# Two FFN units taken in turns at the start of a fused attention and FFN kernel

## The chip, the cores and the metric

The kernel runs on one core of one Trainium2 chip, so its time is that core's device time in microseconds (us), and lower is better. The reported time is the median of unprofiled and profiled executions; the span in a profile is some 2 us shorter. Ratios are computed as the mean time of one kernel's fast runs over that of the other's of the same rounds, so they are not quite the ratios of the medians quoted.

## The reference, cut to what matters

Four batches of 12416 tokens of 128 channels. First an attention block with 32 inducing points, then a SwiGLU FFN with an RMS norm ahead of it:

```python
def mab(q, kv):
    s = scale * (q @ kv.transpose(0, 2, 1))
    s = s - s.max(-1, keepdims=True)
    a = np.exp(s)
    a /= a.sum(-1, keepdims=True) + 1e-09
    return a @ kv
h = mab(I, x)                      # I: the 32 inducing points
attn_out = mab(x, h)
...
rms = np.sqrt(np.mean(x * x, axis=-1, keepdims=True) + 1e-06)
xn = x / rms * rms_g
g = xn @ w_gate                    # 128 -> 1536
silu = g * (1.0 / (1.0 + np.exp(-g)))
return (silu * (xn @ w_val) @ w_out).astype(np.float32)
```

The FFN's weights arrive as 64-bit floats, and the kernel rounds them to 32 bits on the chip.

## The kernel before: the parts that matter here

The token stream is cut into 100 units of up to 512 tokens. A unit is twelve slots (j), one for each 128 of the 1536 FFN channels. In a slot, TensorE makes a gate product g and a value product v from the unit's tile a, ScalarE makes silu(g), VectorE makes u = silu * v, and TensorE adds u's product with w_out to acc a few slots later. Some slots split u in high and low parts instead (three cheaper products, on xn tiles). All attention work of the next batch is hung into these slots by slot number.

```python
for j in range(NJ):
    g = ps_gv.tile([P, 512], F32, name="gv", tag="gv")
    nc.tensor.matmul(g[:, 0:T], sg[:, ts(j, P)], a[:, 0:T], start=True, stop=True)
    sl = silp.tile([P, 512], F32, name="silu")
    nc.scalar.activation(sl[:, 0:T], g[:, 0:T], AF.Silu)
    products(j)                    # acc += u_of_an_earlier_slot @ w_out
    v = ps_gv.tile([P, 512], F32, name="gv", tag="gv")
    nc.tensor.matmul(v[:, 0:T], sv[:, ts(j, P)], a[:, 0:T], start=True, stop=True)
    t = up.tile([P, 512], F32, name="u")
    nc.vector.tensor_tensor(out=t[:, 0:T], in0=sl[:, 0:T], in1=v[:, 0:T], op=ALU.mult)
    steps(j)
```

Before the first slot stands a serial front: load x, transpose, scores, maxima, exponentials, h, the second scores, the norm, and the split of the first unit's a. The first units also need the weights rounded: nine chunks of 512 channels, each by four VectorE operations, two of ScalarE and one of GpSimd.

```python
def parts(clamp=False):
    ...
    nc.vector.tensor_scalar(out=e[:], in0=high, scalar1=20, scalar2=0x7FF,
                            op0=ALU.logical_shift_right, op1=ALU.bitwise_and)
    ...
    nc.vector.tensor_scalar(out=f[:], in0=high, scalar1=0xFFFFF, scalar2=None, op0=ALU.bitwise_and)
def join():
    nc.vector.scalar_tensor_tensor(out=e[:], in0=st["high"], scalar=-(1 << 31), in1=e[:], ...)   # sign
    nc.vector.scalar_tensor_tensor(out=f[:], in0=st["low"].bitcast(U32), scalar=2.0 ** -52, in1=f[:], ...)
    nc.gpsimd.tensor_tensor(out=st["dst"], in0=f[:], in1=e.bitcast(F32)[:], op=ALU.mult)
    put()
...
pool("once", 1); pool("halves", 1); astk = pool("astk", 2)     # ..., hi and lo, a
third = pool("third", 1); silp = pool("silp", 3); up = pool("up", LAG + 3)   # hs, silu, u
```

## Time and profile before

| | before |
|---|---|
| time, median of 4 runs | 1694.65 us (1693.44 to 1695.56) |
| TensorE busy | 98% of the span |
| first FFN matmul | 59.85 us |
| product u of slot 30 | 120.22 us |
| last u (slot 1199) | 1688.11 us |

The table is to be read as three stretches: a serial front of 60 us, an FFN start that is starved of weights for some 30 us, and 1550 us in which TensorE is full. The lines are in the prediction. Slots are counted from 0 by the 1200 products u; that makes the same slot of two kernels comparable.

### The profile page before, as it was taken

The page shows a single profiled execution, that of the slowest core. Times are in us where ns is not written, and L with a number is a line of the kernel's source. Part 1 is how long each engine was busy: PE and PEld are TensorE (multiplying, and loading weights), DVE is VectorE, ACT ScalarE, POOL GpSimd, SP SyncE. Part 2 cuts the span into 40 slices and gives each one's busy share as a digit, 9 for nine tenths or more (in the row PEclk, how much of TensorE's full clock was granted, in tenths as well). Part 3 has the DMA queues.
Part 4 walks back from the last instruction along what each step waited for, and adds up shares of the span by engine and source line. Part 5 has one row for each costly group of instructions (what it writes and reads, how often), then busy time and mean ns, then how long its engine had stood idle before and what let it go on. Part 6 is the DMA issues. An engine that isn't in the chain of part 4 may idle for free.

```text
span 1694.8 us, 23289 instructions
## 1 busy us (share of the span) xinstructions
PE 1661.3 (98%) x6798; PEld 1041.8 (61%) x6798; DVE 1167.6 (69%) x1941; ACT 1236.8 (73%) x2213; POOL 1158.5 (68%) x926
## 2 busy tenths in 40 slices
PE   9799999999999999999999999999999999999998
PEld 7445565655576666665556666566556666666666
DVE  4767876676667776667666787666767666666665
ACT  4446777676787777776678777777677888788886
POOL 1216775776578776676757877577657878878884
PEclk9899999999999999999999999999999999999999
DMA  7344432534354332434336324163211111111111
GB/s 263 75 68 76 69 83 57 123 75 71 55 80 69 47 65 55 105 75 91 63 59 91 57 35 87 29 132 79 56 30 33 35 37 33 33 37 37 32 37 24
DMA packets 389358, 112.64 MB, mean 66 GB/s; under 512 B 365136, under 2 KB 369776, under 8 KB 386672
## 3 DMA queue, kind: packets, MB, share of 16 engines
q1 hardware_dynamic: 388944, 111.02, 33.5%
q8 instruction: 54, 0.88, 0.2%
q14 instruction: 72, 0.59, 0.1%
q10 hardware_dynamic: 288, 0.15, 0.0%
HBM read 53.95 MB, written 27.00 MB: 48 GB/s over the span
## 4 chain that ended last, share of the span: by engine, by line
PE 92%; ACT 2%; DVE 2%; issue 2%; POOL 1%; DMA 1%; ACTq 0%; SPq 0%; DVEq 0%; POOLq 0%
PE acc L564 42%; PE gv L614 16%; PE gv L619 15%; PE u L582 5%; PE u L580 5%; PE mm L310 3%; PE mm L485 1%; PE mm L368 1%; DVE u L621 1%; PE gv L301 1%; ACT silu L616 1%; DMA xn<-in_x_dram 1%; ACT L616 1%; PE gv L310 0%; PE acc L181 0%
## 5 line engine op out<-in xcount | busy, mean ns | idle before, releaser
L621 DVE TENSOR_TENSOR u<-silu,gv 128x512 f32<-128x512 f32 (+2 forms) x1200 | 788.4, 664 | 472.8 <-PE gv L619 239.2
L616 ACT ACTIVATE silu<-gv 128x512 f32<-128x512 f32 (+2 forms) x1200 | 699.1, 584 | 371.0 <-PE gv L614 341.5
L564 PE MATMUL acc<-u,wo 128*128 128x512 f32 (+2 forms) x1600 | 793.7, 580 | 3.6 <-DVE u L621 2.2
L619 PE MATMUL gv<-a,sv 128*128 128x512 f32 (+2 forms) x1200 | 766.0, 638 | 3.8 <-DVE u L621 3.6
L602 POOL TENSOR_TENSOR xn<-u,xn 128x512 fp32r<-128x512 f32 (+2 forms) x400 | 504.9, 1262 | 365.7 <-ACT xn L601 331.2
L607 POOL TENSOR_TENSOR xn<-hs,u 128x512 fp32r<-128x512 f32 (+2 forms) x400 | 503.9, 1260 | 37.7 <-ACT hs L606 35.2
L614 PE MATMUL gv<-a,sg 128*128 128x512 f32 (+2 forms) x1200 | 488.9, 407 | 9.0 <-ACT silu L616 6.3
L614 PEld LDWEIGHTS gv<-a,sg 128*128 128x128 f32 x1200 | 227.2, 189 | 246.8 <-ACT silu L616 122.2
L619 PEld LDWEIGHTS gv<-a,sv 128*128 128x128 f32 x1200 | 227.2, 189 | 199.9 <-issue 136.0
L564 PEld LDWEIGHTS acc<-u,wo 128*128 128x128 f32 x1600 | 298.6, 189 | 83.0 <-issue 19.0
L601 ACT ACTIVATE xn<-u 128x512 fp32r<-128x512 f32 (+2 forms) x400 | 247.8, 620 | 26.8 <-DVE u L621 24.9
L606 ACT ACTIVATE hs<-xn 128x512 f32<-128x512 f32 (+2 forms) x400 | 246.8, 617 | 5.5 <-POOL xn L607 4.0
L564 PE MATMUL acc<-xn,xn 128*128 128x512 f32 (+2 forms) x400 | 156.1, 390 | 4.6 <-POOL xn L607 4.6
L582 PE MATMUL u<-xn,xn 128*128 128x512 f32 (+2 forms) x400 | 155.8, 389 | 0.0
L580 PE MATMUL u<-xn,xn 128*128 128x512 f32 (+2 forms) x400 | 154.4, 386 | 0.0
L564 PEld LDWEIGHTS acc<-xn,xn 128*128 128x128 f32 x400 | 75.0, 187 | 23.9 <-POOL xn L607 8.5
L500 POOL TENSOR_TENSOR rs<-ms,mhalf 128x16 f32<-128x16 f32 (+2 forms) x28 | 75.6, 2698 | 14.6 <-DVE ms L498 12.8
L580 PEld LDWEIGHTS u<-xn,xn 128*128 128x128 f32 x400 | 75.2, 188 | 16.3 <-issue 0.7
L582 PEld LDWEIGHTS u<-xn,xn 128*128 128x128 f32 x400 | 75.1, 188 | 16.2
L573 DVE STREAM_TRANSPOSE o<-o 128x512 f32<-128x512 f32 (+2 forms) x97 | 67.7, 698 | 3.4
L572 DVE TENSOR_TENSOR o<-acc,o 128x512 f32<-128x512 f32 (+2 forms) x97 | 64.9, 669 | 0.1
L585 ACT ACTIVATE o<-u 128x512 f32<-128x512 f32 (+2 forms) x97 | 56.5, 582 | 0.0
(152 smaller groups left out, 732.9 us busy)
## 6 DMA issues: line engine op xcount, KB each, us to landing
out_dram<-o SPq DMA_DIRECT2D x320, 64.0 KB, 2.0
xT<-in_x_dram SPq DMA_DIRECT2D x60, 256.0 KB, 5.1
xn<-in_x_dram SPq DMA_DIRECT2D x60, 256.0 KB, 4.6
a<-hi SPq DMA_DIRECT2D x160, 64.0 KB, 2.0
a<-lo SPq DMA_DIRECT2D x158, 64.0 KB, 2.0
w<-w SPq DMA_DIRECT2D x22, 256.0 KB, 3.1
xn<-in_x_dram SPq DMA_DIRECT2D x5, 1024.0 KB, 11.4
out_dram<-o SPq DMA_DIRECT2D x64, 60.0 KB, 2.0
```

Source lines behind the costliest of these rows:

```text
L500: nc.gpsimd.tensor_tensor(out=rs, in0=ms, in1=mhalf[rows, 0:n], op=ALU.pow)
L564: nc.tensor.matmul(acc[:, 0:T], lhsT, rhs, start=st["left"] == NJ, stop=st["left"] == 1)
L580: nc.tensor.matmul(ups[:, 0:T], w[:, i, :], hi, start=st["k"] == nk, stop=False)
L582: nc.tensor.matmul(ups[:, 0:T], w[:, NK + i, :], lo, start=False, stop=not st["k"])
L601: nc.scalar.activation(hi, v, AF.Copy, scale=1.0 - 2.0 ** -13)
L602: nc.gpsimd.tensor_tensor(out=lo, in0=v, in1=hi.bitcast(F32), op=ALU.subtract)
L606: nc.scalar.activation(hs[:, 0:T], hi.bitcast(F32), AF.Copy, scale=1.0 + 2.0 ** -12)
L607: nc.gpsimd.tensor_tensor(out=d, in0=hs[:, 0:T], in1=v, op=ALU.subtract)
L614: nc.tensor.matmul(g[:, 0:T], sg[:, ts(j, P)], a[:, 0:T], start=True, stop=True)
L616: nc.scalar.activation(sl[:, 0:T], g[:, 0:T], AF.Silu)
L619: nc.tensor.matmul(v[:, 0:T], sv[:, ts(j, P)], a[:, 0:T], start=True, stop=True)
L621: nc.vector.tensor_tensor(out=t[:, 0:T], in0=sl[:, 0:T], in1=v[:, 0:T], op=ALU.mult)
```

## The change

Its intent is to shorten the front and take the stalls out of the FFN's start: x's first set comes in pieces with fewer weights between the sets, there are fewer filler matmuls, h is divided by a 128x1 reciprocal, the first unit's a is made by two selecting matmuls instead of four DMA copies, the first two units take turns so that each 512-channel chunk serves eight slots, and a chunk's rounding is dealt over four slots.

```diff
+            for t0, t1 in (((0, R), (R, 2 * R), (2 * R, n)) if not s else ((0, n),)):
+                nc.sync.dma_start(out=t[:, t0:t1, :], in_=d[:, t0:t1, :])
...
+    sel = const.tile([P, 2, R, m], F32R, name="sel")
...
-            rec = once.tile([P, P], F32, name="rec")
-            nc.vector.reciprocal(out=rec[:], in_=ps[:, P:2 * P])
+            rl = st["rl"] = small.tile([P, 1], F32, name="rl")
+            nc.vector.reciprocal(out=rl[:], in_=ps[:, 0:1])
...
+    def spread(b, u):
...
+        for k, half in enumerate((hi, lo)):
+            nc.tensor.matmul(ps[:, 0:w], sel[:, k, :, :].rearrange("p k m -> p (k m)"), half[:, 0:w],
+                             start=not k, stop=bool(k))
+        a = moving[b, u] = astk.tile([P, 512], F32R, name="a")
+        nc.scalar.copy(out=a[:, 0:w], in_=ps[:, 0:w])
...
-    warm(6)
+    warm(4)
     f["max2"]()
-    warm(4)
+    warm(3)
     f["max3"]()
-    warm(12)
+    warm(8)
...
+            for k, one in ((0, (1, 1)), (3, (2, 1)), (7, (0, 2)), (10, (1, 2)), (13, (2, 2))):
+                for j, name in ((0, "power"), (1, "power_number"), (1, "upper"), (2, "upper_number"), (2, "sign"), (3, "lower")):
+                    add(k + j, weight[one][name])
...
+        order = [(u, j) for u in range(NU) for j in range(NJ)]
+        if not b:
+            order[:2 * NJ] = sorted(order[:2 * NJ], key=lambda one: (one[1] // R, one))
```

sel is a new tile of 1024 B per partition early in SBUF, and rec (512 B) goes while rl comes.

## The prediction

> **What bounds the kernel now.** I read the page first (TensorE busy 98% of the span), then the busy times by stretch, then TensorE's waits on either side of 141 us, and last the chain that ended last, for the first 65 us.
>
> ```profile
> 59.50:90.48 30.98, 23.67 (x58) 10.98 (x58) 23.60 (x35) 13.64 (x24) 6.78 (x6) 0.83 0.42 69
> 90.48:117.77 27.29, 27.29 (x105) 12.94 (x101) 21.21 (x41) 10.04 (x17) 5.69 (x6) 1.00 0.47 77
> ```
>
> Columns: stretch, length, busy time and instructions of PE, weight load, VectorE (DVE), ScalarE (ACT), GpSimd (POOL), granted clock, DMA share, GB/s. In the first 31 us of the FFN TensorE issues 58 matmuls at a clock of 0.83, in the next 27 us 105 at 1.00. So the FFN's start is starved and its sequel is full. TensorE's waits, from 59 to 141 us and then from 141 us to the end:
>
> ```profile
> PE gv L619 <- DVE u L621: 3.0, 1, 3.0
> PE acc L564 <- POOL xn L607: 2.7, 1, 2.7
> PE gv L614 <- DMA a<-lo: 2.4, 1, 2.4
> PE mm L451 <- POOL silu L263: 1.9, 1, 1.9
> PE acc L564 <- POOL wo L263: 1.2, 1, 1.2
> ```
> ```profile
> PE gv L614 <- ACT silu L616: 6.1, 9, 1.0
> PE acc L564 <- DVE u L621: 1.9, 7, 0.7
> PE acc L564 <- POOL xn L607: 1.9, 3, 0.6
> ```
>
> Each line: who waited for whom, us in total, times, longest. After 141 us the listed waits come to some 10 us in 1550, and the change touches nothing there. What can be won lies before 141 us: the path to the first FFN matmul at 59.85 us, and the stalls behind it. On that path, the chain says:
>
> ```profile
> 28.48 1.53 PE acc L181 x12
> 30.12 0.89 PE acc L181 x8
> 31.02 0.31 PE gv L331 x2
> 31.32 2.88 PE acc L181 x24
> 34.20 5.58 PE gv L368 x194
> 39.78 1.09 PE acc L181 x8
> 41.09 0.24 PE gv L383 x2
> 41.35 0.97 DVE rec L385
> 42.35 0.30 DVE hT L387
> ...
> 56.09 0.70 DVE lo L517
> 56.82 0.60 ACTq L529
> 57.46 0.80 ACTq L529
> ```
>
> L181 is the filler matmuls that keep TensorE busy: four times they themselves are on the path. The reciprocal is 0.97 us on 128x128 numbers, and the split (lo) is followed by two DMA issues, then by the landing, before L614 begins at 59.85.
>
> **What the Trainium skill says.** "TensorE: Matmul & The Clock Gate", section "What's actually happening": the array runs at half clock after an idle window of about 3.4 us and recovers after a busy one. The trace agrees in kind: the starved stretch was granted 0.83. "SBUF — State Buffer", section "SBUF: two separate sides": VectorE and GpSimd share a port pair as an exclusive lock, so the later one is blocked for the whole instruction of the other. The trace shows it in the rounding of weights:
>
> ```profile
> 61.01 1.38 POOL L263 TENSOR_TENSOR silu<-o,we 128x512 f32<-128x512 f32 x1 [6.89 <-DVE o L261]
> 61.19 1.63 DVE L243 TENSOR_SCALAR o<-sc 128x512 int32<-128x512 int32 x1
> ```
>
> The same L243 takes 0.42 us where GpSimd is idle; here it ends just after GpSimd. "VectorE: DVE Perf Modes", section "Mode 2×_2P — use both read ports for one tensor", says why tensor_scalar runs at twice the rate of a two-tensor operation: 0.42 against 0.69 us here. "DMA: Bandwidth & Descriptors", section "Anatomy of one DMA — SWDGE (gpsimd) path", gives about 2.0 us fixed for one DMA on GpSimd's path; these 64 KB copies, on a hardware queue, also land after a median 2.0 us.
>
> **The change part by part.** First, x's loads. Set 0 comes in three pieces, and half a megabyte of weights (w_gate's first chunk) no longer stands ahead of set 1. Set 1 is the one x wait of TensorE (2.4 us, until 11.16). At the 426 GB/s moved from 10 to 20 us, 512 KB are 1.2 us. Afterwards the sets are paced by TensorE (2.9 us each, 1.90 for transposes and 1.00 for scores), so the gain is kept: 1.3 us, with the pieces.
>
> Second, fillers. Six to four, four to three, twelve to eight: the first transpose of the maxima could start at 29.5 (its vector input is ready at 29.44) rather than 29.85, and the sums L368 could start when VectorE's first transpose ends at 33.1, not at 34.2. The sums are 5.6 us of TensorE work, the transposes 0.62 us each, so an earlier start is an earlier end: 1.2 us in all.
>
> Third, h's normalisation. From the end of the sums (39.78) to the scores (42.69) it takes 2.91 us now: copy, filler, two products, reciprocal, multiply. New: fold_l and a 128x1 reciprocal come beside the sums; then divide 0.29, one matmul 0.24, copy 0.29, and four handovers of 0.05: 1.02 us. Gain 1.9.
>
> The chain of VectorE from the scores to the split stays as it is (42.69 to 56.79), and the rounding put into it fits its gaps: the sign step (0.6) under the 1.1 us scores, lower under the 0.64 us exponential, and sign, two stack_low and two of parts(0,1), 2.65 us in all, under GpSimd's 2.93 us power. So the split ends at 56.8 - 4.4 = 52.4.
>
> Fourth, spread instead of gather for the first unit: now 59.85 - 56.79 = 3.06 us; new, one matmul to its result 0.4, a ScalarE copy 0.6 and handovers: 1.1. Gain 2.0; first FFN matmul at 53.5, 6.4 us earlier.
>
> Fifth, slots. Up to the gate matmul of slot 30 (at 117.77, 25 output products done) TensorE needs 60 gate and value matmuls at 0.23 = 13.8, 25 products at 0.86 = 21.5, six sets of scores 5.5, three stacked-weight products at 1.1 = 3.3: 44.1 us. It took 57.9, so 13.8 us were stall or low clock. After, all but two stacked-weight products (w_gate and w_val, chunk 0) lie behind the start, four, so 45.2 us. Taking two units in turns needs a new channel chunk every 8 slots instead of every 4, and each chunk's steps are dealt over four slots. What stalls remain comes from VectorE in the first 16 slots: 16 products u at 0.62 = 9.9, five chunks at 1.94 (0.36 and 0.61 twice each, back to back) = 9.7, the last steps of two chunks 1.8, four stack_low 2.6: 24.0 us, and about four waits on the lock, 0.7 each: some 27. TensorE wants 7.4 + 14 x 0.86 + 4.4 = 23.8 there. So I allow 3.2 of stall, and 1.3 for filling the pipeline: 49.7 us against 57.9, gain 8.2. The second unit's copies (four issues at 0.6, landing 2.0, after a raw fetch of 0.4 that waits for lower) should be there 5.5 us after the split, about when slot 4 wants them.
>
> Sum: 1.3 + 1.2 + 1.9 + 2.0 + 8.2 = 14.6 us. The exponential at slot 30 (two table loads of 1.28) and the stall on the first split product (2.7) keep their slots and stay. 1694.5 - 14.6 = 1680.
>
> **The rivals.** One: VectorE takes TensorE's place as the bound of the first 16 slots, with the lock hitting every chunk (five waits of 1.2 us) and each late step delaying a u in VectorE's order. For it: 24.0 against 23.8 is no margin. Against it: the order puts only one fast operation behind each lower, like the one that starts just ahead of GpSimd at 60.85 and takes 0.42. It would cost 4 to 5 us more: 1684.5.
>
> Two: the front gain is hidden. If set 1 or a later set comes no earlier, or the shorter fillers leave the array at half clock (set 1's sixteen transposes took 3.44 us against 1.90 for the next), up to 2.5 us of the front go: 1682.5.
>
> Three: the stall vanishes completely, as the slots flow at TensorE's own pace and never lose clock; then 4.5 us more are won, 1675.5. Against it speaks the same VectorE sum.
>
> Four: the whole gain is given back later, as a different phase of engines and DMA in the 1550 us behind. For it, only that TensorE has waits on ScalarE there; against, that all work there is tied to slot numbers, unchanged from slot 24.
>
> **Range and chances.** Front terms are sums of measured pieces (6.4, give or take 1.5); the slots' term is the uncertain one (8.2, give or take 3). Together about 3.3: an 8-in-10 range of 1676 to 1684.5. Over 2% faster would be 34 us: more than the front stalls hold in all; 2% slower would need a new stall larger than any there. Both 1 to 2%.
>
> **What would show it.** First gate matmul near 53.5 us; reciprocal of one column; TensorE's wait on the DMA of lo gone; slot 30's gate matmul near 103 us; granted clock near 1.00 from 60 to 90 us; VectorE at 9 tenths in that stretch. I am wrong if TensorE shows several waits of over 1 us on u, on a stack_low or on a (the second unit's copies), or if the difference between the kernels at slot 30 is not that at the end.

## The result, and the profile after

The changed kernel takes 1690.9 us (1690.13 to 1691.17, 4 runs) against 1694.65: 3.75 us less, ratio 0.9978 with a 95% interval of 0.996 to 0.9995. The predicted 1680 and its range (1676 to 1684.5) are missed.

Busy times of the changed kernel in the stretches shown before, with the same columns:

```profile
59.50:90.48 30.98, 28.11 (x84) 13.66 (x83) 26.03 (x46) 17.81 (x32) 6.66 (x5) 1.00 0.43 91
90.48:117.77 27.29, 26.82 (x99) 12.08 (x98) 21.84 (x38) 13.93 (x20) 5.80 (x6) 1.00 0.67 97
```

The starved stretch now holds 84 matmuls instead of 58, at full clock. TensorE's longest waits from 54 to 141 us, then from 141 us to the end:

```profile
PE acc L607 <- POOL xn L650: 2.7, 1, 2.7
PE gv L563 <- DVE hi L540: 1.7, 1, 1.7
PE acc L607 <- POOL wo L283: 1.2, 1, 1.2
PE mm L475 <- POOL hs L283: 0.7, 1, 0.7
```
```profile
PE gv L657 <- ACT silu L659: 6.0, 9, 1.0
PE acc L607 <- DVE u L664: 1.9, 7, 0.7
PE acc L607 <- POOL xn L650: 1.8, 3, 0.6
```

The 3.0 us on u and the 2.4 us on the DMA of lo are gone, and the waits of the long stretch are the same as before. The front's chain around h's normalisation, answering to the lines with the 128x128 reciprocal, from the timeline of TensorE:

```profile
37.60 0.41 PE L388 MATMUL gv<-xn,u 128*32 128x128 f32 x4
38.47 0.49 PE L409 MATMUL gv<-fold,hl 128*128 128x128 f32 x2 [0.46 <-DVE hl L404]
39.34 1.07 PE L330 MATMUL gv<-xT,hT 128*32 128x512 f32 x8 [0.38 <-DVE hT L411]
```

From the end of the sums (38.01) to the scores (39.34) it is 1.33 us, where it was 2.91.

All this says that the start was shortened. The products u of slot 40 and of slot 1199, of the kernel before and then of the changed one:

```profile
141.14 0.69 DVE L621 TENSOR_TENSOR u<-silu,gv 128x512 f32<-128x512 f32 x1 [1.56 <-PE gv L619]
1688.11 0.42 DVE L621 TENSOR_TENSOR u<-silu,gv 128x256 f32<-128x256 f32 x1 [0.25 <-PE gv L619]
```
```profile
130.16 0.69 DVE L664 TENSOR_TENSOR u<-silu,gv 128x512 f32<-128x512 f32 x1 [1.68 <-PE gv L662]
1681.78 0.42 DVE L664 TENSOR_TENSOR u<-silu,gv 128x256 f32<-128x256 f32 x1 [0.25 <-PE gv L662]
```

Matched by slot, the two profiles of record differ by 10.99 us at slot 30 and by 10.98 at slot 40. At the last slot they differ by 6.33. So 4.65 us went away in a stretch where both kernels have full engines and the same waits, and evenly: 10.50 at slot 200, 9.21 at 500, 7.90 at 800, 6.79 at 1100.

### The profile page after: what moved, and what is told of

Its sections match the earlier page's. It is cut to its first block, busy times and chain, and to the rows that moved or that the text cites. A ratio compares the mean times of both kernels' runs of the same rounds, so it can differ in the third digit from the quotient of the medians.

```text
span 1688.5 us, 23205 instructions
## 1 busy us (share of the span) xinstructions
PE 1660.7 (98%) x6756; PEld 1036.6 (61%) x6756; DVE 1166.2 (69%) x1941; ACT 1237.4 (73%) x2216; POOL 1159.4 (69%) x931
## 4 chain that ended last, share of the span: by engine, by line
PE 90%; ACT 2%; issue 1%; POOL 1%; DVE 1%; DVEq 0%; POOLq 0%; ACTq 0%
PE acc L607 42%; PE gv L657 17%; PE gv L662 16%; PE u L625 5%; PE u L623 5%; PE mm L330 3%; PE mm L509 1%; PE mm L388 1%; DVE u L664 1%; ACT silu L659 1%; ACT L659 1%; PE mm L461 0%; ACT L448 0%; POOL xn L650 0%; ACT sc L448 0%
```

## The experiments

Sixteen kernels ran, all of them correct. Kernels 1 to 4, 5 to 8, 9 to 12 and 13 to 16 shared a chip.

**Is the even loss the chip or the code?** First the two kernels themselves, without any edit.

> The changed kernel, unaltered, on the same chip and in the same rounds as the kernel before. Up to slot 30 the profiles of record differ by 10.97 us (124.67 against 113.70 us at the same product u), at the end by 6.33 us (last u), and the medians by 3.75 us. The 4.6 us go at an even rate over 1550 us. Theory CHIP: that is a difference between two chips or executions in the pace of full TensorE, not of the kernels; then here the changed kernel is 10 to 11.5 us faster than before, and the difference of the profiles stays level from slot 40 to the end. Theory CODE: the change makes TensorE's full stretch slower by some 4 ns a slot; then here it is 4 to 6.5 us faster, and the difference declines again.

> The kernel before against itself, in the same rounds, as a control of what an equal kernel shows. Both theories: within 1 us of before. Theory CHIP also says that the profile of this run and that of c1_after_again have the same time from slot 40 to slot 1200; theory CODE says 4 to 5 us less here.

Measured: c1 1691.26 us (ratio 0.998, interval 0.9967 to 0.9992), c2 1694.71, the kernel before in the same rounds 1694.93. It is the code. From slot 42 to the last slot, c2 first and then c1:

```profile
141.78:1686.06 1544.28, 1533.80 (x6045) 963.51 (x6044) 1074.03 (x1762) 1171.43 (x2101) 1129.11 (x896) 1.00 0.33 61
```
```profile
133.35:1682.30 1548.95, 1538.62 (x6045) 963.31 (x6044) 1074.40 (x1765) 1170.93 (x2101) 1129.71 (x896) 1.00 0.31 61
```

The same 6045 matmuls at the same granted clock take 4.67 us longer, and TensorE's busy time grows by 4.8 with it. No wait is added: the matmuls stand further apart. Take the slots from 42 on in which TensorE has no attention work. Where it makes the gate and value products and three split products (331 slots), the distance from one gate matmul to the next is 1139.2 ns on average in c2 and 1146.3 in c1; with two plain products in place of the three (665 slots), it is 1307.3 and 1310.2. The compiled programs from unit 2 on have the same instructions, in the same order with the same waits, but for h's normalisation. What differs is where tiles lie and which buffer of a pool comes on which slot.

The same pair shows a second, smaller thing. From slot 36 to slot 40, c2 and then c1:

```profile
130.99:139.14 8.15, 5.47 (x19) 3.20 (x19) 5.17 (x9) 3.50 (x6) 5.82 (x4) 1.00 0.09 20
```
```profile
120.90:130.70 9.80, 7.11 (x19) 3.92 (x19) 5.16 (x8) 3.49 (x6) 5.83 (x4) 0.83 0.14 32
```

Behind the wait on the first split product (2.7 us in both), c1 has one window of 3.413 us at half clock and c2 has none. The profile of record of the kernel before had it too. Of the 11 profiles of kernels with the old front, 4 show it (9.8 us) and 7 don't (8.15 us); of the 7 with the new front, all do.

**Parts undone.** c3 puts the DMA copies back, c4 the order of units.

```diff
-    spread(0, 0)
+    gather(0, 0)
...
+            queue = nc.scalar if (b, u) == (0, 0) and k % 2 else nc.sync
```

> The change with one part undone: the first unit's a is again made by four DMA copies (two from ScalarE's queue) instead of two selecting matmuls and a ScalarE copy. First matmul of the FFN at 55.42 us in the changed kernel, 1.27 us after the split's end, against 3.07 before. Theory PATH (the spread is on the path): 1.5 to 2.0 us slower than c1_after_again. Rival SLACK (VectorE, busy with the last roundings behind the split, would have held the first slots anyway): under 0.7 us slower.

Measured: 1696.86 us, 5.6 us slower than c1, far above both theories. TensorE's wait in c3:

```profile
PE gv L658 <- DMA a<-hi: 7.4, 1, 7.4
```

The first gate matmul is at 61.27 us instead of 56.02. In this order the copies on the Sync queue stand behind a fetch of raw weights that waits for VectorE's last rounding step; they are issued from 56.48 us on, and from 56.66 us, within that wait, TensorE's clock is at half for 10.24 us (three windows). So the spread is on the path, but c3 is no clean measure of it: the trace of record is (3.06 us from the split's end to the first gate matmul before, 1.27 after).

```diff
-            order[:2 * NJ] = sorted(order[:2 * NJ], key=lambda one: (one[1] // R, one))
+            pass
...
-            for k, one in ((0, (1, 1)), (3, (2, 1)), (7, (0, 2)), (10, (1, 2)), (13, (2, 2))):
+            for one, at in (((1, 1), (0, 0, 0, 1, 1, 2)), ((2, 1), (1, 2, 2, 3, 3, 4)), ((0, 2), (2, 3, 3, 4, 4, 5)),
+                            ((1, 2), (4, 5, 5, 6, 6, 6)), ((2, 2), (5, 6, 6, 7, 7, 8))):
...
-            for k, *one in ((2, 0, 1), (5, 1, 1), (12, 0, 2), (15, 1, 2)):
+            for k, *one in ((1, 0, 1), (3, 1, 1), (6, 0, 2), (7, 1, 2)):
```

> The change with the turns undone: units in sequence, and the same steps of rounding packed into slots 0 to 8, as chunk 1 is wanted at slot 4 and chunk 2 at slot 8. Wrong results are not expected. Theory TURNS (dealing the rounding out over more slots is what removed the stalls): VectorE has some 24 us of work in the first 12 to 16 slots, so chunk 2 comes at the pace of VectorE, and the run is 3 to 7 us slower than c1_after_again. Rival: the finer steps alone did it, under 1.5 us slower.

Measured: 1699.3 us, 8.0 us slower than c1; slots 0 to 30 take 60.82 us instead of 52.15. It is more than the range expected. TensorE's waits in c4:

```profile
PE mm L475 <- POOL hs L283: 3.1, 1, 3.1
PE acc L607 <- POOL wo L283: 2.8, 2, 1.6
PE acc L607 <- POOL xn L650: 2.7, 1, 2.7
PE mm L475 <- POOL w L283: 2.5, 2, 1.6
```

Three of the four lines are chunks that come too late from GpSimd, the last step of rounding. They sum to 8.4 us; in the changed kernel the same lines sum to 2.5. So the changed start lives from the turns and from the dealing over four slots. c4 had to undo both at once, since chunks are wanted twice as often without turns; their shares are not separated.

**What takes the 4.6 us?** Where tiles lie, or the rotation of buffers.

```diff
+    const.tile([P, 256], F32, name="pad")          # c5, on the kernel before, at sel's place
```
```diff
-    sel = const.tile([P, 2, R, m], F32R, name="sel")      # c6, on the changed kernel
+    sel = third.tile([P, 512], F32R, name="hs")[:, 0:2 * P].rearrange("p (k q m) -> p k q m", k=2, m=m)
...
-            rl = st["rl"] = small.tile([P, 1], F32, name="rl")
+            rl = st["rl"] = small.tile([P, 1], F32, name="mx")
...
+            if not b:
+                once.tile([P, P], F32, name="rec")
```
```diff
+            if not b:                               # c7, on the kernel before, ahead of rec
+                once.tile([P, 144], F32, name="pad")
```

> The kernel before with one unused tile of 1024 B per partition at the place where the change puts sel, so that all tiles behind it lie 1024 B higher; no instruction is added. From unit 2 on, the changed kernel and the one before have the same instructions in the same order with the same waits (but for h's normalisation), yet the slots of the changed one are longer by 3.6 ns (slots 60 to 600) and 5.4 ns (900 to 1188) on average, with a pattern by slot that repeats to the nanosecond in every kernel derived from it. Theory PLACES: the tiles' addresses in SBUF set that. Then this one is slower than before by 2 to 7 us, at an even rate over the slots, with nothing lost before slot 30. Rival ROTATION: it comes from which buffer of a pool (silu, a, PSUM banks) falls on which slot, or from the state in which the front leaves the engines; then this one is within 0.7 us of before at every slot.

> The changed kernel with the addresses of the kernel before: sel lies in the one buffer of hs, which nothing else needs so early, rl in mx's buffers, and an unused 512 B tile stands where rec was. Rotation of buffers stays that of the change. Theory PLACES: the loss over the slots is gone; the gain of some 10.5 to 11 us at slot 40 stays to the end, and the run is 4 to 5.5 us faster than c1_after_again, about 1686 us. Rival ROTATION: within 0.7 us of c1_after_again (1691).

> The kernel before with an unused tile of 576 B ahead of rec, so that only hT, hg, hi, lo, a, hs, silu, u and o lie 576 B higher, as in the changed kernel, while xn (the split weights and products), sg and sv stay. Theory PLACES, if it is a, u and silu that matter: 2 to 5 us slower than before. If it is xn, sg and sv against the rest that matter: under 1 us. Rival ROTATION: no change.

Measured: c5 1694.73 us (ratio 1.0002, interval 0.9989 to 1.0014), c6 1685.1 (0.9944, 0.9932 to 0.9957), c7 1699.84 (1.0031, 1.0017 to 1.0044), with before at 1694.92. A move of everything by 1024 B costs nothing, so c5 missed what the theory said of it. A move of the upper tiles by 576 B costs what the change lost. The changed kernel with the old addresses keeps its gain. These are the products u of slot 40 and slot 1199 in c6, with the start in the first column:

```profile
129.02 0.69 DVE L666 TENSOR_TENSOR u<-silu,gv 128x512 f32<-128x512 f32 x1 [0.63 <-PE gv L664]
1675.75 0.42 DVE L666 TENSOR_TENSOR u<-silu,gv 128x256 f32<-128x256 f32 x1 [0.24 <-PE gv L664]
```

That is 1546.73 us, as before (1546.97 in the profile of record), where the changed kernel takes 1551.62. So the theory of rotation fell, for c6 keeps the change's rotation.

Then one tile and one distance at a time, on the kernel before:

```diff
+    padp = pool("padp", 1); padp.tile([P, 144], F32, name="pad2")   # c9: 576 B ahead of silu
+    # c10: 576 B ahead of rec, 448 B ahead of silu; c11: 512 B ahead of rec; c12: 64 B ahead of rec
+    # c13: 64 B ahead of hs, 960 B behind it; c14: 64 B ahead of a, 960 B behind it
+    # c15: 32 B ahead of a, 992 B behind it
```

> The kernel before with 576 B of unused room between hs and silu: silu, u and o lie 576 B higher, all else (a too) as before. c7, with a moved too, lost 4.8 us over slots 40 to 1199. If silu and u decide: the same 4.8 us here. If a decides: 0. If it is a's place relative to u's: a loss again, of any size up to 5 us.

> The kernel before with hi, lo, a and hs 576 B higher, and silu, u and o 1024 B higher, which c5 showed to be harmless as far as all moves together. If a (read by TensorE for two of every slot's matmuls) decides: 4.8 us lost over the slots. If silu and u decide: 0.

> As c7, but 512 B instead of 576. If the place modulo 128 decides (a and u lie at an odd multiple of 64 B before and at an even one in the changed kernel): 0 here and the loss of 4.8 us in c12. If the half of a 1024 B stretch decides: the loss here.

> As c7, but 64 B instead of 576. If the place modulo 128 decides: 4.8 us lost over slots 40 to 1199, as in c7. If the half of a 1024 B stretch decides: 0.

> The kernel before with hs alone 64 B higher, and silu, u and o 1024 B higher. From slot 40 to the last, the kernel before takes 1546.95 us, c12 (all from rec on 64 B higher) 1551.80, c10 (hi, lo, a, hs) 1550.24. If a decides: 1546.9 to 1547.2 here. If hs decides: 1550 to 1551.

> The kernel before with a alone 64 B higher, and hs, silu, u and o 1024 B higher. If a decides: 1550.0 to 1550.5 us from slot 40 to the last, as in c10. If hs, hi or lo does: 1547.

> The kernel before with a alone 32 B higher, and hs, silu, u and o 1024 B higher; a then lies at 96 modulo 128 (before: 64, changed kernel: 0). If it is 128 B stretches that matter, the worst place being 0: 1546 to 1548.5 us. If only 64 modulo 128 is good: 1550 or more.

Measured:

| kernel | moved | start of a modulo 128 B | slots 40 to 1199, us | time, us |
|---|---|---|---|---|
| c2 (before) | nothing | 64 | 1546.92 | 1694.71 |
| c5 | all behind sel's place by 1024 B | 64 | 1547.01 | 1694.73 |
| c9 | silu, u, o by 576 B | 64 | 1546.93 | 1694.83 |
| c11 | all from rec on by 512 B | 64 | 1546.94 | 1695.0 |
| c13 | hs by 64 B | 64 | 1546.82 | one look |
| c15 | a by 32 B | 96 | 1546.51 | one look |
| c10 | hi, lo, a, hs by 576 B | 0 | 1550.24 | 1698.58 |
| c14 | a by 64 B | 0 | 1550.46 | one look |
| c12 | all from rec on by 64 B | 0 | 1551.80 | 1698.59 |
| c7 | all from rec on by 576 B | 0 | 1551.80 | 1699.84 |
| c1 (changed) | sel, rec, rl | 0 | 1551.60 | 1691.26 |
| c6 (changed, old places) | nothing | 64 | 1546.73 | 1685.1 |

The two products u of c14, slots 40 and 1199:

```profile
141.18 0.69 DVE L625 TENSOR_TENSOR u<-silu,gv 128x512 f32<-128x512 f32 x1 [1.70 <-PE gv L623]
1691.64 0.42 DVE L625 TENSOR_TENSOR u<-silu,gv 128x256 f32<-128x256 f32 x1 [0.24 <-PE gv L623]
```

c10, c13, c14 and c15 also move what lies behind the padded tiles by 1024 B, which c5 had shown to cost nothing. The addresses of a are those of the compiled programs (195520 and 197568 before, 196096 and 198144 in the changed kernel). The tile is a, the moving operand of the gate and value matmuls. Where it starts on a multiple of 128 B, the full stretch is 3.3 to 3.5 us longer; where silu, u and o lie so too, 4.7 to 4.9. With those there alone (c9) nothing is lost, so the two don't simply add, and why is left open, as is what in the hardware makes a's place count. Only starts at 0, 64 and 96 modulo 128 were tried.

**A few waits more.** c8 takes three waits out of c6, c16 only the last of the three.

```diff
-    weight[2, 0]["sign"]()            # c8: sign behind the two stack_low
...
-    warm(26)
+    warm(31)                          # c8
...
-(13, (2, 2))
+(12, (2, 2))                          # c8 and c16
```

> c6_after_places with three waits of the changed kernel's first 87 us taken away: the sign step of w_out's first chunk behind the two stack_low instead of ahead of GpSimd's power (which took 3.29 us instead of 2.92), five more fillers ahead of the selecting matmuls (TensorE sat 1.69 us idle there and had half clock in the first slots), and w_out's last chunk rounded one slot earlier (a product waited 1.24 us for it). If each wait is on the path: 0.3 + 0.7 + 1.2 = 2.2 us faster than c6_after_places. Rival: VectorE holds the same slots anyway; under 0.7 us.

> c6_after_places with w_out's last chunk rounded one slot earlier and nothing else. In the profile of c8 the slots from 17 on came 1.4 us closer to slot 16 than in c6. If that wait is on the path: 1.2 to 1.5 us faster than c6 (1685.1), so about 1683.7. Rival: VectorE gives it back before slot 30: under 0.4 us.

Measured: c8 1684.91 us (ratio 0.9942), c16 1685.73 (0.994), against 1685.1 for c6 (0.9944). In the profiles the edits do what they should: slots 0 to 30 take 50.61 (c8) and 50.56 us (c16) where c6 has 52.14, and the power in c8 is back at 2.92 us. The times don't show it; the intervals are some 4 us wide, and the front of single profiles differs as much (the u of slot 0 is at 56.17, 57.70 and 58.82 us in c6, c8 and c16, though c6 and c16 have the same program up to there). Whether these waits are worth anything in the whole time is not settled. c6 and c8 beat both kernels: 9.8 us and 10.0 us less than before, of the same rounds.

## Why the prediction was wrong, step by step

The profiles of record, between the same two events each:

| step | predicted gain, us | measured, us |
|---|---|---|
| x's loads (start of the first fillers, 28.41 to 27.37) | 1.3 | 1.04 |
| fillers (start of the sums, 34.13 to 31.73, less the step above) | 1.2 | 1.36 |
| h's normalisation (start of the scores, 42.69 to 39.34, less the two above) | 1.9 | 0.95 |
| VectorE's chain, scores to split (14.10 to 14.81) | 0 | -0.71 |
| spread (split to first gate matmul, 3.06 to 1.27) | 2.0 | 1.79 |
| slots, first gate matmul to u of slot 30 (60.37 to 53.81) | 8.2 | 6.56 |
| sum at slot 30 | 14.6 | 10.99 |
| slots 40 to 1199 (1546.97 to 1551.62) | 0 | -4.65 |

**The step that failed** is the sentence that after 141 us "the change touches nothing there", and the argument against rival four, that all work there is tied to slot numbers. The order, the operations and the waits are indeed the same, and rival four's outcome came without its reason, for no phase of engines or DMA is in it. The prediction's own sign of being wrong, that the difference at slot 30 is not that at the end, came true. The change allocated sel and rl and dropped rec, and that moved a from 64 to 0 modulo 128 B. c7 shows the loss without any of the change's instructions, c14 most of it with a alone, and c6 the change without the loss.

**The terms that were mis-sized.** The normalisation itself came to 1.33 us instead of 1.02. But the sums ahead of it took 6.28 us (31.73 to 38.01) instead of 5.58, which the prediction had not allowed for: the fold_l matmul stands between them, and the last sums start behind it. In the chain that "stays as it is", two things got longer: GpSimd's power from 2.92 to 3.29 us, and VectorE's z product came 0.41 us later behind its matmul. The first, in the timeline of the changed kernel:

```profile
48.03 0.68 DVE L275 SCALAR_TENSOR_TENSOR we<-sc,we 128x512 int32<-128x512 int32 x1
```
```profile
48.20 3.29 POOL L524 TENSOR_TENSOR rs<-ms,mhalf 128x16 f32<-128x16 f32 x1 [3.61 <-DVE ms L522]
```

The sign step with two SBUF inputs is under way when the power starts. In c8, where it comes later, the power took 2.92 us again. The prediction had placed the step "under" the power as if it were free, though it names the lock a few lines above. The 0.41 us of z were not explained. In the slots, the stalls left were those listed: 1.24 us for w_out's last chunk and 1.3 for gate and value chunks. The first is about the shortfall of 1.64 us: c16, without it, takes 52.25 us from the first gate matmul to the u of slot 30, where the 8.2 us predicted would have left 52.17. There was also a window of half clock (54.83 to 58.24 us), which began after TensorE had sat 1.69 us idle ahead of the selecting matmuls. In c6 that same idle time brought no such window, and in c16, the same program up to there, it did, so it is chance whether it comes. It cost these slots nothing: they took 53.81 us with it and 53.84 in c6 without, where TensorE waited 1.1 us for u instead of 0.2.

**What was right.** The spread, the fillers, the x loads and the disappearance of the wait on lo's DMA came as worked out. VectorE was busy for 26.03 of 30.98 us in the first slots, a little under the nine tenths predicted. Rival one did not come to pass as described: the waits were on single chunks, none on u of over 0.3 us. Rival two came near in size, not in cause: the first gate matmul came 4.43 us earlier instead of 6.4, for the reasons above, while x's sets and the shorter fillers kept their gain. Of rival three nothing showed.

Both errors count. The gain at slot 30 is 10.99 us where 14.6 was predicted, and with a's place put right (c6) the kernel took 1685.1 us, 0.6 above the range; a's place alone takes 4.65. That leaves 2.6 us to the measured 3.75, and most of it lies in the profile of record of the kernel before: that execution took 1696.75 us, 2.1 above the median, with the window of half clock (1.65 us) that 7 of the 11 profiles of the old front don't have. c1 and c2 give 10.11 us at slot 30, 8.44 at slot 40 and 3.76 at the end.

## What to carry to other kernels

When a change adds, drops or resizes a tile, compare the addresses of the operands of the costliest loop before and after it, and match the two traces by a counted event: a difference that shrinks evenly over a loop with unchanged instructions pointed here to the loop's operands, not to the edit one was looking at. Here 64 bytes of padding were worth more than most parts of the change. A step put "under" another engine's operation is free only if the two don't lock each other out.

## What the Trainium skill lacked or had wrong

- No page says that the place of a moving operand sets TensorE's pace. "SBUF — State Buffer", section "Operand start alignment", says of its own measurements that they are about legality and timed nothing. Here a on a multiple of 128 B made slots 40 to 1199 take 1550.46 us (c14) instead of 1546.92 (c2); 96 B past one, 1546.51 (c15).
- The same page, section "SBUF: two separate sides", has the shared port pair held for the whole of an instruction, the loser blocked. For GpSimd's product of two 128x512 tiles that agrees with the trace. For its power on 128x16 it does not: while that ran from 48.20 to 51.49 us in the changed kernel, VectorE's tensor_scalar at 50.06 and 50.40 us took 0.43 and 0.42 us, as when GpSimd is idle.
- "TensorE: Matmul & The Clock Gate", section "What's actually happening", gives the window of about 3.4 us; the traces agree (windows of 3.413 us at half clock). It also says that an idle window brings the half clock, but not what counts as idle. Here a wait of 2.7 us, shorter than a window, was followed by one in 11 of 18 profiles and by none in 7.
